# Delta-rule attention and MLP: Gram blocks written in the transpose's order, K loaded 32 wide, group 1 solved in 32 steps

## The chip, the cores and the metric

One core of a Trainium2 chip runs the whole program. The metric is the time of one execution in device microseconds; lower is better. Three runs of the kernel before took 690.51, 685.59 and 689.33 us (median 689.33). A fourth execution was profiled and took 684.56 us, of which 682.8 lie between its first and its last instruction.

## The reference, cut to what matters

```python
def _attn_ref(q, k, v, beta):                    # each (4, 8, 768, 48), beta (4, 8, 768)
    k_n = k / (np.linalg.norm(k, axis=-1, keepdims=True) + 1e-06)
    for t in range(S):
        y[:, :, t] = np.einsum('bhd,bhde->bhe', q[:, :, t], state)
        v_old = np.einsum('bhde,bhd->bhe', state, kt)
        state = state + bt[:, :, :, None] * np.einsum('bhd,bhe->bhde', kt, vt - v_old)

def _moe_ref(x, w_in, w_out):                    # x (3072, 384), w_in (384, 2048)
    h = x @ w_in
    sp = np.where(h > 20.0, h, np.log1p(np.exp(np.minimum(h, 20.0))))
    g = h * np.tanh(sp)
    return g @ w_out
```

The attention's output, with heads and width put side by side, is the `x` of the MLP.

## The kernel before

**Attention in chunks.** The 768 steps are cut into 12 chunks of 64, and two chunks make a group (g = 0 to 5). The 32 pairs of batch and head lie as two halves of 16. Within a chunk the recurrence is a triangular system. For each group the function `early(g)` builds it: TensorE multiplies K by itself (the Gram blocks, tile `pg`, L1752), VectorE masks the result out of PSUM into a tile `d` (L1755), four pieces a group, and ScalarE copies the other half of each piece to `at` (L1757). One VectorE transpose turns `d` into `gt` (L1763), so that each pair's block lies on a partition of its own. From the diagonal come the norms of K: `ss` on VectorE, then Ln and Exp on ScalarE (L1773, L1774), then a reciprocal and the factors `nb`, for which the transposed `betaT` is needed. Then the system is solved in place, on VectorE: a product `pr` (L1806) and a sum into `gt` (L1808) for each step, each of a few dozen to 256 elements a partition, each waiting for the one before.

**Two ways of solving.** `TN["fg"]` is the number of groups that are solved in two blocks of 16 steps (`split` in the code), before 2: groups 0 and 1. Their solve has 28 instructions. The blocks are then put together by TensorE in `merge(n)`, one for each chunk: matmuls `ma` (L1860, 64 a chunk), a ScalarE copy `ym` (L1862), matmuls `mb` (L1871, 64 a chunk), a VectorE sum into `tt` (L1874) and a transpose `tn` (L1876). Each of the two matmul blocks of a chunk comes in two halves by row, so that the order names `ma2`, `ma3` and `mb2`, `mb3` for the chunks of group 1. The split solve ends in the transposes `tu` (L1816) and `tt` (L1818). Groups 2 to 5 are solved in one block of 32 with 60 instructions and no merge; they end in `d<-gt` (L1825) and `tn<-gt` (L1829), and GpSimd copies the result to its place in `tt` (`place`, L1841).

**What uses it.** Per chunk n, TensorE then runs `ta` (with the solved block), `tb` (with `tn`), `gq`, `pz`, and `py` with `ps`, the output and the carried state (all L1936). `py2_0` is the first output block of chunk 2. The outputs are transposed and evicted to `x` (L2061 to L2065).

**The MLP.** An `h` tile is 18 matmuls (L2089) into one of two PSUM buffers, then a chain that alternates between ScalarE and VectorE: exp (L2103), min and add (L2104), square, ln and exp (L2105 to L2107), `e<-e,h` on VectorE (L2108, which frees the `h` buffer), a cast to `g` (L2109) and a remainder on VectorE (L2110). The second product adds up in `acc` (L2126, 12 matmuls for each `g`). The weights come as float64, read as pairs of int32, and are converted to high and low parts in the first 150 us by all engines (`convert`, L1665 to L1697).

**Loads.** K of a chunk comes in eight DMAs (`load_src`), for each half two 32 wide and two 16 wide (the width of 48 in two parts). The 16 columns beside a 16-wide part are cleared by `memset` (L1710) ahead of the load, on VectorE for chunks 0 and 1 and on GpSimd for the others.

**What sets the order.** All engines run in the order in which the program is written (`manual_schedule`). That order comes from the table `TT`, which gives each step of each piece of work (such as `early1`, `merge2`, `g1.0.0`) a position. Where several are named, as in `acc(g2.1.0)`, it is the MLP's token block, half and step.

Of the kernel before, what the change touches and what calls it, by code (L numbers as in the profile page):

```python
# [28 lines left out]
def bcast_in(ap, n):  # L29
# [21 lines left out]
    'scale_v(0,1)': [27],
    'cv1': [35, 68, 70, 104, 119, 98, 131, 144, 145],
    'warm8.0': [36],
    'loado1': [43],
    'loadq': [47],
    'scale_v(0,0)': [48],
    'warm11.5': [49],
    'loadi2': [50],
    'loadk2': [51],
    'loado0': [52],  # L60
    'merge0': [62, 71, 99, 101],
    'loado2': [63],
    'loado5': [64],
    'loado3': [65],
    'loadi4': [66],
    'loadx': [67],
    'turn_q(0,0,(0,))': [72],
    'cv2': [73, 110, 111, 112, 165, 156, 177, 194, 178],
    'turn_q(0,1,(1,))': [74],
# [2328 lines left out]
```

## Time and profile before

| what | value |
|---|---|
| runs of the kernel | 690.51, 685.59, 689.33 us, median 689.33 |
| the profiled execution | 684.56 us; its span 682.8 us, mean granted clock 0.970 |
| TensorE (PE) busy | 635.3 us, 93% of the span |
| VectorE (DVE) busy | 489.9 us, 72% |
| ScalarE (ACT) busy | 430.3 us, 63% |
| GpSimd (POOL) busy | 72.1 us, 11% |

"Busy" is the time in which at least one instruction of the engine is under way; what is left of the span is the engine's idle time. A row of the timeline begins with start and duration in us, and ends in brackets with the idle time of the engine ahead of it and the instruction that ended that time; "issue" there means that nothing in the profile explains the wait. The granted clock is the share of full speed that TensorE was given in a stretch. An average over the span hides stages: VectorE is busy for 72% over all, but for 95% from 140 to 160 us.

### The profile page before, as it was taken

To read this page: it belongs to the slowest core of one execution; us is meant where nothing else is said; L and a number is where in the kernel's file an instruction comes from. 1 tells how busy PE (TensorE), PEld (TensorE's weight loads), DVE (VectorE), ACT (ScalarE), POOL (GpSimd) and SP (SyncE) were. 2 spreads that over 40 slices of the span, in tenths; PEclk is the share of its full clock that TensorE was granted. 3 is DMA by queue.
4 is the path that set the end of the run, shared out by engine and by line. 5 is a ranking of instruction groups with operands and counts; after the bars stand their busy time and mean duration, and the time that the engine had idled before them with its cause. 6 is when DMAs were issued, how large, how long until landed. Compare 5 with 4: busy or idle time off the path is not lost.

```text
span 682.8 us, 23514 instructions
## 1 busy us (share of the span) xinstructions
PE 635.3 (93%) x10203; PEld 577.8 (85%) x10203; DVE 489.9 (72%) x1042; ACT 430.3 (63%) x802; POOL 72.1 (11%) x119
## 2 busy tenths in 40 slices
...
GB/s 154 164 285 216 213 1 26 1 48 49 5 48 49 64 19 45 62 22 56 36 33 53 45 35 42 48 37 26 42 42 35 22 42 48 25 20 7 1 24 23
DMA packets 161510, 37.79 MB, mean 55 GB/s; under 512 B 154720, under 2 KB 157792, under 8 KB 161408
## 3 DMA queue, kind: packets, MB, share of 16 engines
...
q10 hardware_dynamic: 6464, 0.69, 0.8%
...
## 4 chain that ended last, share of the span: by engine, by line
PE 43%; DVE 35%; ACT 8%; issue 6%; DMA 4%; SPq 4%; ACTq 0%; DVEq 0%
PE h L2089 15%; PE acc L2126 15%; DVE gt L1808 5%; DVE pr L1806 5%; DVE e L2108 4%; DVE g L2110 3%; SPq L1621 3%; DVE xx L1987 3%; PE gq L1936 3%; DVE xx L1923 2%; DMA kt<-in_k_dram 2%; DVE gt L1763 2%; DVE e L2104 2%; DMA xx<-in_q_dram 2%; PE pg L1752 2%
## 5 line engine op out<-in xcount | busy, mean ns | idle before, releaser
L2089 PE MATMUL h<-x,wi 128*128 128x256 f32 x1728 | 232.1, 289 | 17.3 <-DVE e L2108 5.4
L2089 PEld LDWEIGHTS h<-x,wi 128*128 128x128 f32 x1728 | 218.9, 192 | 25.2 <-DVE e L2108 6.7
L2126 PE MATMUL acc<-wo,g 128*128 128x384 f32 x1152 | 225.5, 344 | 4.4 <-DVE g L2110 2.2
L2126 PEld LDWEIGHTS acc<-wo,g 128*128 128x128 f32 x1152 | 199.8, 190 | 10.8 <-DVE g L2110 6.1
L2108 DVE SCALAR_TENSOR_TENSOR e<-e,h 128x512 f32<-128x512 f32 x96 | 65.7, 684 | 76.8 <-ACT e L2107 75.3
L2105 ACT ACTIVATE e<-e 128x512 f32<-128x512 f32 x96 | 60.6, 631 | 54.1 <-DVE e L2104 53.3
L2109 ACT CAST g<-e 128x512 fp32r<-128x512 f32 x96 | 59.3, 618 | 48.5 <-DVE e L2108 47.0
L2110 DVE TENSOR_TENSOR g<-e,g 128x512 fp32r<-128x512 f32 x96 | 68.4, 713 | 28.8 <-ACT g L2109 27.7
L2103 ACT ACTIVATE e<-h 128x512 f32<-128x512 f32 x96 | 57.2, 595 | 42.7 <-PE h L2089 34.2
L2107 ACT ACTIVATE e<-e 128x512 f32<-128x512 f32 x96 | 60.6, 632 | 2.7
L2106 ACT ACTIVATE e<-e 128x512 f32<-128x512 f32 x96 | 60.6, 631 | 2.5
L2104 DVE TENSOR_SCALAR e<-e 128x512 f32<-128x512 f32 x96 | 41.6, 435 | 26.2 <-ACT e L2103 25.8
L1808 DVE TENSOR_TENSOR gt<-gt,pr 128x84 f32<-128x84 f32 (+14 forms) x148 | 51.3, 346 | 3.5
L1806 DVE TENSOR_TENSOR pr<-gt 128x84 f32<-128x84 f32 (+14 forms) x148 | 49.8, 337 | 3.5
L1936 PE MATMUL gq<-xx,kt 48*64 48x112 f32 (+1 forms) x768 | 44.5, 260 | 2.2 <-DVE xx L1923 1.3
L1936 PE MATMUL py<-xx 128*64 128x48 f32 x768 | 43.5, 227 | 2.9 <-ACT xx L2009 2.9
L1936 PEld LDWEIGHTS py<-xx 128*64 128x64 f32 x768 | 39.5, 141 | 7.8 <-ACT xx L2009 3.8
L1936 PEld LDWEIGHTS gq<-xx,kt 48*64 48x64 f32 x768 | 38.3, 136 | 4.4 <-DVE xx L1923 2.2
L1987 DVE TENSOR_TENSOR xx<-gq,amask 64x256 f32<-64x256 f32 x96 | 40.2, 418 | 0.7
L1936 PE MATMUL ps<-xx 128*48 128x48 f32 x704 | 39.0, 211 | 0.4 <-DVE xx L1987 0.2
L1936 PEld LDWEIGHTS pz<-vt,tt 64*64 64x64 f32 x768 | 32.7, 135 | 5.1 <-issue 2.9
L1936 PE MATMUL pz<-vt,tt 64*64 64x48 f32 x768 | 36.6, 231 | 0.0
...
## 6 DMA issues: line engine op xcount, KB each, us to landing
...
kt<-in_k_dram SPq DMA_DIRECT2D x44, 64.0 KB, 2.5
...
```

The lines of the kernel that those rows point to most:

```text
L1806: nc.vector.tensor_tensor(out=pv, in0=nj, in1=xj, op=ALU.mult)
L1808: nc.vector.tensor_tensor(out=below, in0=below, in1=pv, op=ALU.add)
L1936: last[:] = [nc.tensor.matmul(*a, start=True, stop=True)]
L1987: nc.vector.tensor_tensor(out=x[r, p4, hh, D:D + C], in0=ps[r, :, d:], in1=bcast_mid(amask[r], 4), op=ALU.mult)
L2089: nc.tensor.matmul(h[:, f2, :], wt["i", f * P // WI * NCH + c][:, i2, f0:f0 + P], x[:, c, :], start=(i == 0), stop=(i == 3 * NCH - 1))
L2105: (0.65, lambda: nc.scalar.activation(e, e, AF.Square)),
L2106: (0.65, lambda: nc.scalar.activation(e, e, AF.Ln, bias=0.5, scale=0.5)),
L2107: (0.7, lambda: nc.scalar.activation(e, e, AF.Exp, scale=-1.0)),
L2108: (0.8, lambda: nc.vector.scalar_tensor_tensor(e, e, -1.0, h, op0=ALU.add, op1=ALU.mult)),
L2109: (0.7, lambda: nc.scalar.copy(out=gg[:, 0], in_=e)),
L2110: (0.8, lambda: eng.tensor_tensor(out=gg[:, 1], in0=e, in1=gg[:, 0], op=ALU.subtract))):
L2126: nc.tensor.matmul(acc[t], gg[:, a, f2, ts_], wt["o", f][:, i2, :], start=(f == 0 and i == 0), stop=(f == NF - 1 and i == 2))
```

## The change

1. For groups that are solved in 32 steps the masked Gram block is written to `d` in the order in which the transpose reads it, so that `gt<-d` reads contiguously; `tn` is transposed from the solved `d`, again contiguously, and no more from `gt`.
2. The 16-wide parts of K (and of Q's chunk 1) are loaded 32 wide, with the first 16 values of the row that follows in memory (`wide_rows`); nothing uses these values. Of the 24 memsets of `kt` only the last chunk's remain, and the two of `q1` go.
3. `fg` is 1: group 1 is solved in 32 steps, like groups 2 to 5. `merge2` and `merge3` are gone; group 1 gets the `d<-gt`, `tn<-d` and placing copies of the later groups, and `ta2` reads `d`.
4. The table `TT` is new throughout (1415 keys for 1425).

```diff
-    TN = dict(tl=4.0, fg=2, pl=[*range(0, 8)], po=8, pg=(), db=2, sp=21, slow=1.4, ab0=(39.5, 1.45), gqe=(2.,2.), ev=0,
+    TN = dict(tl=4.0, fg=1, pl=[*range(0, 8)], po=8, pg=(), db=2, sp=21, slow=1.4, ab0=(39.5, 1.45), gqe=(2.,2.), ev=0,
...
+    def wide_rows(src, hh):
+
+        flat = src.rearrange("hh t (b h) d -> (hh b h t d)", b=2)
+        rows = flat[32:B * H * S * D - (D - 32)].rearrange("(m d) -> m d", d=D)
+        m0 = hh * (NP * S - C)
+        return rows[m0:m0 + NP * S, 0:32].rearrange("(p t) d -> t p d", t=S)
...
+                if ch and n == NS - 1:
+                    nc.gpsimd.memset(dst[64 * (1 - hh) + 32:64 * (1 - hh) + 64, :, :, D - 32:], 0.0)
...
-                    load(dst[r0:r0 + 32, :, tb, :w], src[hh, t0:t0 + 32, :, 32 * ch:32 * ch + w])
+                    if ch and n < NS - 1:
+
+                        load(dst[r0:r0 + 32, :, tb, :], wide_rows(src, hh)[t0 + C * hh:t0 + C * hh + 32])
+                    else:
+                        load(dst[r0:r0 + 32, :, tb, :w], src[hh, t0:t0 + 32, :, 32 * ch:32 * ch + w])
...
-        for r in (slice(32, 64), slice(96, 128)):
-            (nc.vector if n < 2 else nc.gpsimd).memset(kts[n][r, :, :, D - 32:], 0.0)
...
+        dg = dt.rearrange("p a b f -> p (a b f)").rearrange("p (f a b) -> p a b f", a=2, b=NP)
...
-                    nc.vector.tensor_tensor(out=dt[:, t2, pr, :], in0=ps[:, :, 32:],
+                    to = dt[:, t2, pr, :] if split else dg[:, t2, pr, :]
+                    nc.vector.tensor_tensor(out=to, in0=ps[:, :, 32:],
...
-        nc.vector.transpose(gt, dt.rearrange("p a b f -> p f (a b)"))
+        if split:
+            nc.vector.transpose(gt, dt.rearrange("p a b f -> p f (a b)"))
+        else:
+            nc.vector.transpose(gr.rearrange("p a b -> p (a b)")[:, :32 * 32], dt.rearrange("p a b f -> p (a b f)"))
...
-            nc.vector.transpose(tn.rearrange("p a b j -> p j (a b)"), gt.rearrange("p i j -> p j i"))
+            nc.vector.transpose(tn.rearrange("p a b j -> p (a b j)"), dt.rearrange("p a b i -> p (a b i)"))
...
-    put(f"early{1}", early(1), *TN['e1'], *spread(us(1 + TN['s1'][0]), us(1 + TN['s1'][1]), 28), us(1 + TN['f1']), need=("K2",))
-    put(f"merge{2}", merge(2), *(us(1 + t) for t in TN['m2']), need=(f"T{(2) // 2}",))
-    put(f"merge{3}", merge(3), *(us(1 + t) for t in TN['m3']), need=(f"T{(3) // 2}",))
+    put(f"early{1}", early(1), *TN['e1'], *spread(us(1 + TN['s1'][0]), us(1 + TN['s1'][1]) + 10, 60), *(us(1 + TN['s1'][1]) + 11 + i for i in range(4)), need=("K2",))
...
-    'loada': [5],
+    'loada': [53],
```

What the new table does is seen in the order of the engines. First ScalarE, from its first instruction that is no load on: before, one load of its function table stands ahead of the copies to `at` and of Ln and Exp (L1773, L1774), and the copy of `betaT` behind them.

```order
L2200 ACT_TABLE_LOAD
L1757 COPY at_151<-pg_1_185 128x256
L1757 COPY at_151<-pg_0_152 128x256
L1757 COPY at_219<-pg_0_220 128x256
L1757 COPY at_219<-pg_1_261 128x256
L1773 ACTIVATE y_320<-ss_318 128x32
L1774 ACTIVATE y_320<-y_320 128x32
L2191 COPY betaT<-beta 128x192
```

The same place in the changed kernel, where Ln and Exp are L1779 and L1780.

```order
L1760 ACT_TABLE_LOAD
L1760 COPY at_154<-pg_0_155 128x256
L1760 COPY at_154<-pg_1_188 128x256
L1760 COPY at_228<-pg_0_229 128x256
L2197 COPY betaT<-beta 128x192
L1760 COPY at_228<-pg_1_264 128x256
L1779 ACT_TABLE_LOAD
L1779 ACTIVATE y_326<-ss_324 128x32
L1780 ACT_TABLE_LOAD
L1780 ACTIVATE y_326<-y_326 128x32
```

The step that asks for the joint table (`loada`) now comes later than these instructions, so three loads stand here instead of one, two of them between the last copy and Exp; a fourth, the joint table, follows further on (L2206). The second place is VectorE at the end of group 1's solve. Before, the 28 instructions end in L1808, and then:

```order
L1810 TENSOR_TENSOR gt_1954<-gt_1954,bp_2022 128x2x16x16
L1816 STREAM_TRANSPOSE tu_2286<-gt_1954 128x16x32
L1818 STREAM_TRANSPOSE tt_102<-gt_1954 128x32x32
L2104 TENSOR_SCALAR e_1_2260<-e_1_2260 128x512
L1721 STREAM_TRANSPOSE kt_1263<-kt_1263 128x1024
L2108 SCALAR_TENSOR_TENSOR e_1_2260<-e_1_2260,h_1_2241 128x512
L1874 TENSOR_TENSOR tt_102<-tt_102,mb_0_2397 128x8x16
L2104 TENSOR_SCALAR e_2_2310<-e_2_2310 128x512
L1874 TENSOR_TENSOR tt_102<-tt_102,mb_1_2435 128x8x16
```

In the changed kernel 60 instructions end in L1814, and then:

```order
L1816 TENSOR_TENSOR gt_1991<-gt_1991,bp_2047 128x1024
L1831 STREAM_TRANSPOSE d_1515<-gt_1991 128x32x32
L2116 TENSOR_TENSOR g_0_2180<-e_0_2179,g_0_2180 128x512
L1835 STREAM_TRANSPOSE tn_2301<-d_1515 128x1024
L2110 TENSOR_SCALAR e_1_2334<-e_1_2334 128x512
L1722 STREAM_TRANSPOSE kt_1234<-kt_1234 128x1024
L2110 TENSOR_SCALAR e_2_2266<-e_2_2266 128x512
L2114 SCALAR_TENSOR_TENSOR e_1_2334<-e_1_2334,h_1_2315 128x512
L2116 TENSOR_TENSOR g_1_2335<-e_1_2334,g_1_2335 128x512
```

The sums of the merges are gone from between the MLP's instructions, one `g` (L2116, the remainder that the second product reads) stands between the last two transposes, and the two transposes feed `ta2` and `tb2` directly.

## Rows read from the trace of the kernel before

**Rows 1.** The page, part 1: busy time of each engine, share, instructions.
```profile
PE 635.3 (93%) x10203; PEld 577.8 (85%) x10203; DVE 489.9 (72%) x1042; ACT 430.3 (63%) x802; POOL 72.1 (11%) x119
```
**Rows 2.** Windows: stretch, length, busy PE, PEld, DVE, ACT, POOL, clock, DMA, GB/s.
```profile
140.00:160.00 20.00, 14.94 (x207) 13.72 (x208) 19.08 (x50) 8.95 (x16) 0.00 (x0) 0.91 0.36 61
160.00:180.00 20.00, 18.35 (x660) 17.36 (x663) 11.02 (x19) 11.74 (x24) 4.40 (x7) 0.92 0.05 7
```
**Rows 3.** Timeline of VectorE: group 1's solve from its transpose to its end.
```profile
128.92 2.05 DVE L1763 STREAM_TRANSPOSE gt<-d 128x1024 f32<-128x1024 f32 x1
...
156.61 0.69 DVE L1810 TENSOR_TENSOR gt<-gt,bp 128x512 f32<-128x512 f32 x1
157.34 1.06 DVE L1816 STREAM_TRANSPOSE tu<-gt 128x512 f32<-128x512 f32 x1
158.30 1.90 DVE L1818 STREAM_TRANSPOSE tt<-gt 128x1024 f32<-128x1024 f32 x1
```
**Rows 4.** Timeline of TensorE from group 1's merges to the first output block.
```profile
158.54 1.27 PE L1860 MATMUL ma<-tu,d 16*32 16x16 f32 x128 [2.53 <-DVE tu L1816]
159.75 3.91 PE L2126 MATMUL acc<-wo,g 128*128 128x384 f32 x12
...
167.69 1.20 PE L1936 MATMUL ta<-tt,at 32*32 32x32 f32 x64
168.81 2.38 PE L2126 MATMUL acc<-wo,g 128*128 128x384 f32 x12
...
175.04 0.24 PE L1871 MATMUL mb<-tt,ym 32*32 32x16 f32 x5 [1.65 <-issue]
175.21 2.40 PE L2089 MATMUL h<-x,wi 128*128 128x256 f32 x18
...
186.33 0.42 PE L1871 MATMUL mb<-tt,ym 32*32 32x16 f32 x26 [1.49 <-issue]
186.68 0.32 PE L1936 MATMUL py<-xx 128*64 128x48 f32 x4
```
**Rows 5.** Windows of tile ma (PE, PEld, ACT), then of mb (PE, PEld, DVE).
```profile
155.00:190.00 35.00, 2.79 (x256) 2.55 (x256) 0.98 (x4) 0.91 0.13 21
...
155.00:190.00 35.00, 3.12 (x256) 2.66 (x256) 1.15 (x4) 0.91 0.13 21
```
**Rows 6.** Windows of tile pr, the solve's instructions: group 1, then group 2.
```profile
138.00:157.00 19.00, 7.34 (x28) 0.91 0.31 57
190.00:258.00 68.00, 20.18 (x60) 1.00 0.30 47
```
**Rows 7.** Groups by form on VectorE (busy us, mean ns); one timeline row, group 2.
```profile
L1721 DVE STREAM_TRANSPOSE kt<-kt 128x1024 f32<-128x1024 f32 x12 | 14.9, 1240 | 3.0 <-DMA kt<-in_k_dram 2.9
L1829 DVE STREAM_TRANSPOSE tn<-gt 128x1024 f32<-128x1024 f32 x4 | 8.9, 2221 | 0.6 <-PE ta L1936 0.6
...
193.11 1.22 DVE L1790 TENSOR_TENSOR gt<-gt,nb 128x1024 f32<-128x1024 f32 x1
```
**Rows 8.** Group by form on ScalarE, and VectorE's timeline behind group 0's solve.
```profile
L2200 ACT ACT_TABLE_LOAD x1 | 1.3, 1283 | 7.1 <-DMA kt<-in_k_dram 7.1
...
33.20 0.71 DVE L1923 STREAM_TRANSPOSE xx<-xx 64x512 f32<-64x512 f32 x1
```
**Rows 9.** Timeline of TensorE: group 0's mb, ta0, tb0 and the first output.
```profile
41.00 1.30 PE L1871 MATMUL mb<-tt,ym 32*32 32x16 f32 x82 [1.81 <-issue]
...
45.27 0.69 PE L1936 MATMUL ta<-tt,at 32*32 32x32 f32 x18 [1.10 <-issue]
...
51.80 1.20 PE L1936 MATMUL tb<-at,tn 32*32 32x32 f32 x64
...
58.66 0.32 PE L1936 MATMUL py<-xx 128*64 128x48 f32 x2 [0.57 <-ACT xx L2009]
```
**Rows 10.** Waits of TensorE from 187 us on: total us, times, longest.
```profile
PE h L2089 <- DVE e L2108: 4.6, 6, 1.9
PE acc L2126 <- DVE g L2110: 2.2, 4, 0.7
```

More of the change, by code (lines that the diff above doesn't have):

```diff
@@ L51 @@
[L51 to L69, printed above, removed]
@@ new lines @@
+    'early0.1>1': [10],
+    'early0.2>1': [11],
+    'loado2': [12],
+    'loadi1': [15],
+    'loads': [17],
+    'early0.4>1': [18],
+    'turn_beta()': [19],
+    'early0.5>1': [20],
+    'warm8.0': [22],
+    'warm11.5': [24],
+    'loado1': [25],
+    'loadq': [26],
+    'scale_v(0,0)': [27],
+    'cv0': [50, 28, 62, 81, 84, 108, 112, 129, 128],
+    'scale_v(0,1)': [30],
+    'cv1': [31, 52, 61, 92, 106, 85, 130, 139, 140],
+    'loadi2': [34],
+    'loadk2': [37],
+    'cv4': [38, 57, 156, 158, 219, 227, 230, 231, 192],
@@ new lines @@
+    'loada': [53],
+    'turn_q(0,1,(0,))': [54],
+    'turn_q(0,0,(1,))': [55],
+    'loado3': [59],
+    'turn_q(0,0,(0,))': [60],
+    'loado5': [63],
+    'loadi4': [64],
+    'loadx': [65],
+    'loado6': [76],
+    'loado0': [77],
+    'loadi3': [78],
+    'warm30.6': [79],
+    'warm29.5': [80],
+    'merge0': [82, 83, 99, 100],
+    'loado4': [86],
+    'loadi5': [87],
+    'loadp': [88],
+    'gq00': [89],
+    'cv5': [90, 144, 194, 195, 196, 211, 215, 223, 216],
+    'turn_q(0,1,(1,))': [91],
@@ new lines @@
+    'g1.0.6': [456],
+    'g1.0.7.0>1': [457],
+    'ats_y[1,1].0>1': [459],
+    'scale_v(2,0)': [461],
+    'g1.0.6.0>1': [465],
+    'scale_v(2,1)': [466],
+    'g1.0.6.0>2': [467],
+    'g2.0.5': [478],
+    'turn(1,)': [479],
+    'g1.0.6.0>3': [480],
+    'g1.0.6.0>4': [481],
+    'g1.0.6.0>5': [482],
+    'turn(1,).0>3': [483],
+    'ats_gq[2,0]': [484],
+    'turn(1,).0>1': [490],
+    'g1.0.6.0>6': [492],
+    'g1.0.6.0>7': [496],
+    'turn(1,).0>4': [499],
+    'turn(1,).0>2': [510],
@@ new lines @@
+    'g1.0.7.0>2': [518],
+    'g1.0.6.0>8': [524],
+    'g1.1.0': [525],
+    'turn_q(2,1)': [529],
+    'prep(3,)': [530],
+    'g2.0.6': [538],
+    'g1.1.0.0>1': [539],
+    'g1.0.7.0>3': [540],
+    'g1.0.7.0>4': [541],
+    'g1.0.7.0>5': [542],
+    'g1.0.7.0>6': [543],
+    'g1.1.0.0>2': [553],
+    'g1.0.7.0>7': [555],
+    'g1.0.7.0>8': [562],
+    'g1.1.2': [567],
+    'ats_gq[2,0].0>1': [570],
+    'ats_gq[2,0].0>2': [576],
+    'g1.1.0.0>3': [578],
+    'g1.1.0.0>4': [579],
+    'g1.1.0.0>5': [580],
@@ new lines @@
+    'g1.1.0.0>6': [583],
+    'g1.1.0.0>7': [588],
+    'g1.1.0.0>8': [589],
+    'g1.1.2.0>1': [590],
+    'g2.0.7': [592],
+    'g1.1.1': [593],
+    'g2.0.7.0>1': [594],
+    'g2.0.7.0>2': [595],
+    'g2.1.0': [596],
+    'g1.1.1.0>1': [597],
+    'g1.1.1.0>2': [598],
+    'g1.1.1.0>3': [600],
+    'g1.1.1.0>4': [601],
+    'ats_a[2]': [602],
+    'g1.1.1.0>5': [603],
+    'g1.1.2.0>2': [604],
+    'g1.1.2.0>3': [605],
+    'g1.1.1.0>6': [606],
+    'g1.1.1.0>7': [607],
+    'ats_a[2].0>1': [608],
@@ new lines @@
+    'g1.1.1.0>8': [609],
+    'g1.1.2.0>4': [610],
+    'g1.1.3': [611],
+    'g1.1.2.0>5': [612],
+    'g1.1.2.0>6': [613],
+    'g2.1.1': [614],
+    'g1.1.3.0>1': [615],
+    'g1.1.2.0>7': [618],
+    'g1.1.2.0>8': [619],
+    'g1.1.3.0>2': [620],
+    'ats_b[2]': [621],
+    'g1.1.3.0>3': [623],
+    'g1.1.3.0>4': [624],
+    'g1.1.4': [625],
+    'ats_b[2].0>1': [626],
+    'scale_v(3,1)': [629],
+    'g1.1.3.0>5': [630],
+    'g1.1.3.0>6': [631],
+    'g1.1.3.0>7': [632],
+    'g1.1.4.0>1': [633],
@@ new lines @@
+    'g1.1.5.0>8': [702],
+    'g1.1.6.0>5': [703],
+    'g1.1.7': [704],
+    'ats_y[2,1].0>1': [706],
+    'g1.1.6.0>6': [708],
+    'turn(2,)': [709],
+    'g1.1.6.0>7': [710],
+    'ats_b[3]': [714],
+    'g1.1.7.0>1': [715],
+    'turn(2,).0>1': [716],
+    'turn(2,).0>3': [719],
+    'g1.1.6.0>8': [720],
+    'turn(2,).0>4': [722],
+    'turn(2,).0>2': [724],
+    'g1.1.7.0>2': [725],
+    'g1.1.7.0>3': [727],
+    'g1.1.7.0>4': [728],
+    'turn_q(3,1)': [730],
+    'prep(4,)': [731],
+    'ats_b[3].0>1': [732],
@@ new lines @@
+    'g2.1.7.0>1': [765],
+    'g1.2.0.0>6': [766],
+    'ats_y[3,0]': [767],
+    'g1.2.1.0>2': [769],
+    'g1.2.0.0>7': [770],
+    'g2.1.7.0>2': [773],
+    'g1.2.0.0>8': [774],
+    'g1.2.3': [776],
+    'g1.2.1.0>3': [778],
+    'g1.2.1.0>4': [779],
+    'g1.2.1.0>5': [782],
+    'scale_v(4,0)': [783],
+    'g2.2.0': [784],
+    'ats_y[3,0].0>1': [785],
+    'g1.2.1.0>6': [789],
+    'g1.2.1.0>7': [790],
+    'g1.2.3.0>1': [791],
+    'g1.2.1.0>8': [795],
+    'g1.2.3.0>2': [797],
+    'early3.3>1': [801],
@@ new lines @@
+    'g1.2.2': [804],
+    'g1.2.3.0>3': [805],
+    'g1.2.3.0>4': [809],
+    'g1.2.3.0>5': [810],
+    'g2.2.1': [811],
+    'g1.2.2.0>1': [812],
+    'g1.2.3.0>6': [813],
+    'g1.2.2.0>2': [814],
+    'g1.2.3.0>7': [815],
+    'turn_q(4,0)': [816],
+    'early3.2>1': [817],
+    'g1.2.2.0>3': [818],
+    'g1.2.2.0>4': [819],
+    'g1.2.3.0>8': [820],
+    'g1.2.4': [821],
+    'g1.2.2.0>5': [822],
+    'ats_z[3,1]+s_gq[4,0]': [824],
+    'ats_z[3,1]+s_gq[4,0].0>2': [825],
+    'g1.2.2.0>6': [826],
@@ new lines @@
+    'g2.2.3': [851],
+    'g1.2.5.0>3': [853],
+    'g1.2.4.0>7': [854],
+    'g1.2.5.0>4': [856],
+    'g1.2.5.0>5': [857],
+    'ats_a[4].0>1': [858],
+    'turn(3,)': [859],
+    'turn(3,).0>3': [860],
+    'g1.2.4.0>8': [862],
+    'g1.2.6': [864],
+    'turn(3,).0>1': [866],
+    'g1.2.5.0>6': [867],
+    'g1.2.6.0>1': [869],
+    'g2.2.4': [870],
+    'turn(3,).0>4': [871],
+    'turn(3,).0>2': [872],
+    'g1.2.5.0>7': [873],
+    'scale_v(4,1)': [874],
+    'g1.2.6.0>2': [878],
+    'g1.2.5.0>8': [880],
@@ new lines @@
+    'g1.2.7.0>3': [924],
+    'g1.3.0.0>6': [925],
+    'g1.2.7.0>4': [926],
+    'g1.2.7.0>5': [927],
+    'g1.2.7.0>6': [932],
+    'g1.2.7.0>7': [933],
+    'g1.2.7.0>8': [937],
+    'ats_y[4,0]': [938],
+    'scale_v(5,1)': [939],
+    'ats_y[4,0].0>1': [940],
+    'g1.3.1': [941],
+    'g1.3.0.0>7': [942],
+    'g1.3.1.0>1': [943],
+    'g1.3.0.0>8': [945],
+    'g1.3.1.0>2': [946],
+    'g2.2.7': [950],
+    'g2.2.7.0>1': [951],
+    'g1.3.1.0>3': [953],
+    'g1.3.1.0>4': [954],
+    'g1.3.1.0>5': [955],
@@ new lines @@
+    'g1.4.3.0>2': [1129],
+    'g1.4.3.0>3': [1130],
+    'g1.4.4': [1131],
+    'g1.4.3.0>4': [1133],
+    'g1.4.3.0>5': [1134],
+    'g2.4.2': [1136],
+    'g1.4.4.0>1': [1139],
+    'g1.4.3.0>6': [1143],
+    'g1.4.3.0>7': [1144],
+    'g1.4.4.0>2': [1147],
+    'g1.4.4.0>3': [1148],
+    'g1.4.3.0>8': [1151],
+    'g1.4.5': [1152],
+    'ats_y[5,1]': [1153],
+    'g1.4.4.0>4': [1154],
+    'g1.4.4.0>5': [1155],
+    'g1.4.5.0>1': [1157],
+    'g1.4.4.0>6': [1160],
+    'g2.4.3': [1162],
+    'g1.4.4.0>7': [1163],
@@ new lines @@
+    'g1.5.7.0>4': [1359],
+    'g1.5.7.0>5': [1361],
+    'g1.5.6.0>8': [1362],
+    'g1.6.0': [1363],
+    'g1.6.0.0>1': [1364],
+    'g2.5.6': [1365],
+    'g1.5.7.0>6': [1366],
+    'g1.6.0.0>2': [1367],
+    'ats_z[7,0]+s_gq[7,1].0>1': [1368],
+    'g1.6.0.0>3': [1369],
+    'g1.5.7.0>7': [1370],
+    'g1.6.0.0>4': [1371],
+    'g1.6.0.0>5': [1372],
+    'g1.5.7.0>8': [1373],
+    'g1.6.1': [1374],
+    'g2.5.7': [1376],
+    'g1.6.0.0>6': [1377],
+    'g1.6.0.0>7': [1378],
+    'g1.6.1.0>1': [1379],
```

1178 lines of the change are left out of this document (1151 added, 27 removed), and 1372 rows, old and new, of the table TT.

## The prediction

> **What bounds the kernel now.** I read the page first: TensorE (PE) is busy for 93% of the span, VectorE (DVE) for 72% [rows 1]. On that alone one would say that only TensorE's work counts. Then I read the windows of 20 us: from 140 to 160 us VectorE is busy for 19.08 of 20 us and TensorE for 14.94, and in the next 20 us it is the other way round, 11.02 and 18.35 [rows 2]. So the stretch in which the change puts the longer solve has VectorE as its limit until 160 us, and slack on VectorE behind it. The timeline shows what ends there: group 1 is transposed at 128.92 us, and its solve ends with `tt` at 158.30 + 1.90 = 160.20 us [rows 3]. That is 31.3 us, in which VectorE also serves the MLP and converts weights. TensorE waits 2.53 us for `tu`, then runs the merges among MLP work, `ta2` at 167.69 and the first output block of chunk 2, `py2_0`, at 186.68 us, with idle times of 1.65 and 1.49 us ahead of two of the merges' blocks, for which the trace names no instruction [rows 4]. From there the two kernels have the same work on TensorE. I therefore ask when `py2_0` starts in the changed kernel, and what is different behind it.
>
> **What goes.** Group 1's merges hold TensorE for 2.79 + 3.12 = 5.91 us [rows 5], and the three idle times beside them add 2.53 + 1.65 + 1.49 = 5.67 us [rows 4]. At most 11.6 us of TensorE can come free. The memsets of `kt` lie on GpSimd, which is 11% busy [rows 1], or ahead of the first K; I give them nothing, since the work of TensorE behind them starts with K's landing and not with them. If a later K load had waited for GpSimd's memset, there would be a wait of `pg` for it; none of the large waits is one [rows 10], so the bound is about zero on both sides. The 16-wide loads become 32 wide, with as many packets; I give that nothing, for DMA is 36% busy or less at the loads of chunk 3 and later [rows 2].
>
> **What group 1's solve costs.** Its own instructions took 7.34 us in 28 steps; group 2's 60 took 20.18 us [rows 6]: +12.84. The two products with a factor for each row or column are twice as large, 1.22 for 0.69 us each [rows 3, 7]: +1.06. `d<-gt` takes the place of `tu` and `tt`: a transpose with one strided side takes 2.05 us [rows 3], against 1.06 + 1.90: -0.91. The transpose into `gt` now reads contiguously: the one contiguous transpose of this size takes 1.24 us [rows 7], so -0.81. Together 31.3 + 12.84 + 1.06 - 0.91 - 0.81 = 43.5 us from `gt` to `d`, as VectorE is full and other work stands between the steps as before (the order has about as much of it). If VectorE's idle time of that stretch, some 5% [rows 2], is used up, it is 42; so 42 to 43.5, and I take 43.5, since the steps alternate with chains that ScalarE must feed.
>
> **From there to py2_0.** On VectorE a remainder `g` stands right behind `d` (as VectorE's order shows), 0.7 us for its 512 elements as for L1810 [rows 3]; the second product `acc` that waits for it stands ahead of `ta2` on TensorE. That `acc` takes 2.38 us, or 3.91 where TensorE had idled just before it: the same 12 matmuls [rows 4]. In the changed kernel TensorE has little to do for about 20 us ahead of it, since its `h` and `acc` blocks wait for instructions of VectorE that stand between the steps; so 3.9. `ta2` starts at 43.5 + 0.7 + 3.9 = 48.1 us behind `gt`, where it started at 167.69 - 128.92 = 38.8. From `ta2` to `py2_0` it took 186.68 - 167.69 = 19.0 us. Of that go the idle 1.65 + 1.49 and the merge blocks that lie there, 0.7 + 0.8 + 0.9 (a half of `ma` is 0.7 us at 2.79 / 4, a half of `mb` 0.8 at 3.12 / 4, the last a little more), and one `h` block more stands there, 2.40 us [rows 4, 5]: 15.9 us. So `py2_0` comes 64.0 us behind `gt`, where it came 57.8: **+6.2 us**. If all runs at full clock and VectorE's idle time is used, it is +3; if two blocks more run at the slow rate and their `e` chains are late by as much, +9.
>
> **What comes earlier.** Ahead of `gt` two things pull in opposite ways. The order of ScalarE shows two loads of its function table between the last copy and Exp, one of them ahead of Ln, where it may lie beside VectorE's transpose. A load took 1.283 us [rows 8]. One load is on the chain for certain, so +1.3 to +2.6; I take 2.1, since the copy of `betaT` has moved ahead of them too. Into group 0's solve VectorE now takes three transposes of `xx`, 0.71 us each [rows 8], and five conversions of 0.3 to 0.4 us, where it had one: +3.6. Against that, `tb0` stood 51.80 - 45.96 = 5.8 us behind the end of `ta0`, with eight warm-up matmuls and four of a conversion between them [rows 9]. In the new order only two of the latter are left there, and the warm-ups stand behind `tb0`: -3.6. The `gq` blocks no longer wait for those transposes, which have run by then: -2.0. Together +0.1, so that the first output block stays at about 58.7 us [rows 9]; bounds -3 (the unexplained idle times of 1.81 and 1.10 us go too [rows 9]) and +3 (both loads on the chain and half of these shifts lost). Then half of a merge of chunk 1 stands behind the first `h`, not ahead of it, 0.7 us by [rows 5], and between the first `e` of the MLP and `gt` of group 1 VectorE's order holds 47.1 us of work by the mean of each form, for 49.5. So `gt` starts 3.0 us earlier, and `py2_0` is late by 6.2 - 3.0 = **+3.2 us**.
>
> The Trainium skill ("ScalarE: Activation LUTs", section "What ACT_TABLE_LOAD costs") gives about 1283 ns for the load, as the trace, and a drain of about as long again with it, 2.66 us for a switch. No drain can be seen in this trace, which has one load at the start. By the Trainium skill the sum would be higher by about 2.8 us for two such loads on the chain, an estimate from that section.
>
> **What comes back behind py2_0.** In groups 2 to 5 the transpose into `gt` gives 0.81 us each, `tn` 2.22 - 1.24 = 0.98 [rows 3, 7]: 1.8 us of VectorE a group, 7.2 in all. The masked evictions, four a group, now write with a stride. The trace has no such instruction. Below, it costs nothing, as the trace has no reason for a loss in a two-input operation; above, what a stride costs a transpose, 0.81 us per 1024 elements, so 0.2 for 256 and 0.8 a group. I take half. Then 5.6 us of VectorE are saved, off the path except where TensorE waits for VectorE: the two largest waits of that stretch are 4.6 and 2.2 us [rows 10]. I give the change **-2.5 us** there, with bounds 0 and -5. The work that hides the rest is TensorE's MLP, which is full.
>
> The Trainium skill ("SBUF — State Buffer", section "Specifications (TRN2)") has lines of 16 bytes, with a penalty for each step to a new line. By that section's rule the evictions, which step 128 bytes, would pay the upper bound, and the first part of the change would only move the price of `gt` from the transpose to the evictions. The sum would then be +1 us higher. The strided transposes agree with the rule: 2.05 for 1.24 us.
>
> **The sum.** +3.2 - 2.5 = +0.7 us. The profiled execution took 684.56 us, so 685.3 for one like it. The three runs have a median of 689.33, and the mean of all four is 687.5; the sum on that is 688.2. I predict **688 us**, about the same. About 1% (6.9 us) is what a measurement of this kernel can tell from no change.
>
> **Rivals.** (A) *The merges come out whole.* If the longer solve hides in VectorE's slack, the 11.6 us of TensorE go: 687.5 - 11.6 = 676. For it: VectorE is idle for 9 of 20 us right behind the solve [rows 2], and the early bound of -3. Against: the slack lies behind the solve, and `ta2` stands behind it. A middle form, with half of them, gives 681. (B) *The solve is the new bound and the clock falls with it* (the other side). VectorE's extra 12.2 us up to `d` lie ahead of `ta2`; TensorE waits, and the `h` and `acc` blocks behind the wait run at the slow rate, 1.5 us more each [rows 4]. With +9 there, no gain ahead and none behind: 687.5 + 9 = 696.5. It decides from `py2_0` at 193.6 us on, if nothing comes back later. For it: 19.08 of 20 us [rows 2]. Against: only three blocks stand there. (C) *The parts ahead of `gt` go wrong*: table loads, full solve, late K, +3 each side of nothing: 691 to 692, no verdict. That the change doesn't do what it says is excluded by the order of the instructions.
>
> **Chances.** Forecast with (C), 682.4 to 696.2 us: 0.52. (A), below: 0.31. (B), above: 0.17. The range goes from 676 to 698, from all of (A) to a little above (B); the likeliest case by itself has 683 to 694.
>
> **What would show it.** Right: no `ma2`, `mb2`; 60 steps in about 20 us; `gt` of group 1 near 126 us, `d` 42 to 44 us behind it, `ta2` near 174 and `py2_0` near 190; Ln about 2 us later behind `ss`, with loads of 1.28 us; `gt` and `tn` transposes at 1.24 us. Wrong: `py2_0` ahead of 184 (A) or behind 193 (B); evictions at more than 0.6 us; idle time of TensorE behind `py2_0` that differs by more than 5 us.

## The result, and the profile after

The changed kernel takes 682.04 us (median of 10 runs, 677.92 to 685.82), the kernel before 688.68 us on the same chip (10 runs, 685.59 to 690.51). The ratio is **0.9894, with an interval of 0.9865 to 0.9923**: faster by 1.1%, where "about the same" was forecast at 688 us. The profiled execution took 679.45 us, 5.1 us less than that of before.

The page of the changed kernel, part 1, beside [rows 1]:

```profile
PE 625.0 (92%) x9687; PEld 575.4 (85%) x9691; DVE 486.6 (72%) x1064; ACT 433.6 (64%) x801; POOL 62.8 (9%) x100
```

TensorE has 516 matmuls and 10 us of busy time less, VectorE 3 us less. The windows that answer [rows 2]:

```profile
140.00:160.00 20.00, 11.16 (x55) 10.52 (x56) 19.18 (x50) 5.83 (x10) 0.00 (x0) 0.79 0.03 5
160.00:180.00 20.00, 15.21 (x234) 13.73 (x236) 15.55 (x30) 9.69 (x17) 6.59 (x9) 0.87 0.26 47
```

VectorE is as full as before until 160 us and for longer behind it (15.55 us for 11.02), and TensorE stands still for almost 9 of the 20 us, where it stood for 5. So this stretch got worse. VectorE's timeline, for [rows 3]:

```profile
126.19 1.24 DVE L1769 STREAM_TRANSPOSE gt<-d 128x1024 f32<-128x1024 f32 x1
...
167.13 2.02 DVE L1831 STREAM_TRANSPOSE d<-gt 128x1024 f32<-128x1024 f32 x1
...
169.57 1.22 DVE L1835 STREAM_TRANSPOSE tn<-d 128x1024 f32<-128x1024 f32 x1
```

Group 1 starts 2.7 us earlier, and 43.0 us lie from `gt` to the end of `d`. TensorE's timeline, for [rows 4]:

```profile
165.31 3.91 PE L2095 MATMUL h<-x,wi 128*128 128x256 f32 x18 [3.63 <-DVE e L2114]
169.05 0.51 PE L2132 MATMUL acc<-wo,g 128*128 128x384 f32 x2
169.72 2.02 PE L2132 MATMUL acc<-wo,g 128*128 128x384 f32 x10 [0.15 <-DVE g L2116]
171.67 1.20 PE L1942 MATMUL ta<-d,at 32*32 32x32 f32 x64
173.87 2.40 PE L2095 MATMUL h<-x,wi 128*128 128x256 f32 x18 [1.00 <-DVE e L2114]
...
185.71 2.26 PE L1754 MATMUL pg<-kt 48*32 48x64 f32 x64 [1.82 <-issue]
...
192.81 0.32 PE L1942 MATMUL py<-xx 128*64 128x48 f32 x4
```

`py2_0` starts at 192.8 us, 6.1 us later than before. The span ends 5.1 us earlier. So between these two executions the changed kernel loses 6 us up to this block and gains 11 behind it; how much of the 6 is chance is seen below. The granted clock around the block, from two windows of 5 us (the number ahead of the DMA share):

```profile
185.00:190.00 5.00, 4.29 (x116) 4.15 (x118) 2.65 (x6) 2.07 (x5) 0.00 (x0) 0.58 0.01 3
190.00:195.00 5.00, 5.00 (x173) 4.58 (x171) 2.88 (x6) 2.15 (x5) 0.00 (x0) 0.74 0.01 3
```

TensorE ran for some of this time at the lower of its two levels, 1.2 GHz, after the idle time of 1.82 us; the kernel before has 0.72 and 0.94 in the same two windows. Behind 193 us its waits are smaller than [rows 10]:

```profile
PE h L2095 <- DVE e L2114: 2.1, 3, 0.9
PE h L2095 <- DVE x L2071: 1.4, 2, 1.3
PE acc L2132 <- DVE g L2116: 1.3, 3, 0.5
```

The rest of the document asks where those 11 us come from. One table serves for this. From each trace I take the first matmul of `py2_0`, that of `py6_0` (the first output block of chunk 6) and the end of TensorE's work. "Order" says whose table of positions holds behind `py2_0`.

| kernel | order behind | parts | py2_0 at | py2_0 to py6_0 | py6_0 to end | ratio to before |
|---|---|---|---|---|---|---|
| before | old | none | 186.7 | 193.4 | 298.3 | 1 |
| changed | new | all | 192.8 | 185.2 | 295.3 | 0.9894 |
| b_edits12 | old | 1, 2 | 191.8 | 192.8 | 296.3 | 1.0002 |
| b_fg1 | old | 1, 2, 3 | 199.0 | 191.7 | 297.3 | 1.0125 |
| a_fg2 | new | 1, 2 | 196.8 | 186.8 | 295.8 | 0.9929 |
| a_table | new | all | 192.9 | 185.2 | 298.0 | 0.9901 |
| h_oldfront | new | 1, 2 | 189.9 | 184.5 | 298.0 | 0.9831 |
| h_newfront | old | all | 193.5 | 192.2 | 297.0 | 1.0005 |
| a_oldwrite | new | 2, 3 | 192.7 | 185.9 | 296.3 | 0.9910 |
| a_memset | new | 1, 3 | 190.8 | 185.2 | 297.6 | 0.9900 |
| h_mid | new to py6_0 | 1, 2 | 191.7 | 187.9 | 298.1 | 0.9897 |
| b_accswap | old, 12 blocks moved | 1, 2 | 193.6 | 195.9 | 299.6 | 1.0125 |
| h_three | new | 1, 2 | 185.8 | 187.7 | 297.5 | 0.9818 |
| b_rear | new | none | 191.8 | 187.3 | 296.8 | 0.9852 |

The ratios are of 6 to 12 runs of each changed kernel; the three columns of times are of one execution each. A run more than 1.5% above the fastest of its kernel counts as slow and is left out of the ratio; for b_rear these are 7 of 12 runs, the traced one among them, and with all 12 its ratio (of the means) is 0.990.

The start of the program scatters. b_edits12, h_oldfront, h_mid and b_accswap have the same instructions in the same order up to `py2_0`, and reach it between 189.9 and 193.6 us; the kernel before and b_rear share theirs as well, and reach it at 186.7 and 191.8. So the trace of the kernel before is the earliest of six with the old front, whose mean is 190.9 us. The five executions with the changed kernel's order up to there (changed, a_table, a_oldwrite, a_memset, h_newfront) have a mean of 192.5. The loss ahead of `py2_0` is thus nearer to 2 us than to 6. What scatters lies ahead of `gt` of group 1 (128.9 to 134.4 us in the old front); from there to `py2_0` the old front takes 57.4 to 59.8 us and the changed one 64.1 to 66.6. The stretch from `py2_0` to `py6_0` repeats itself far better. Its windows, in the kernel before, b_edits12 and the changed kernel:

```profile
186.68:380.08 193.40, 182.27 (x3024) 170.61 (x3019) 171.27 (x382) 122.34 (x228) 25.59 (x39) 0.99 0.27 43
191.85:384.67 192.82, 182.06 (x3025) 171.15 (x3020) 168.20 (x383) 122.32 (x228) 20.17 (x29) 0.99 0.28 47
192.81:377.99 185.18, 177.49 (x3025) 169.15 (x3019) 163.60 (x378) 123.37 (x231) 20.01 (x28) 1.00 0.29 49
```

With the same matmuls, TensorE stands still for 11.1, 10.8 and 7.7 us there, so less than half of the 8 us is idle time. The rest is a shorter busy time. The granted clock of 0.99 accounts for up to 2 us of that, by an estimate from these rows; what makes the remainder isn't shown.

### The profile page after: what moved, and what is told of

Read it like the earlier page. It is cut to its first block, busy times and chain, and to the rows that moved or that the text cites. A ratio compares the mean times of both kernels' runs of the same rounds, so it can differ in the third digit from the quotient of the medians.

```text
span 677.7 us, 22475 instructions
## 1 busy us (share of the span) xinstructions
PE 625.0 (92%) x9687; PEld 575.4 (85%) x9691; DVE 486.6 (72%) x1064; ACT 433.6 (64%) x801; POOL 62.8 (9%) x100
## 3 DMA queue, kind: packets, MB, share of 16 engines
q8 instruction: 76, 1.25, 0.8%
## 4 chain that ended last, share of the span: by engine, by line
PE 58%; DVE 26%; issue 5%; SPq 4%; DMA 4%; ACT 3%; DVEq 0%; ACTq 0%
PE h L2095 22%; PE acc L2132 20%; SPq L1611 4%; DVE pr L1812 4%; DVE gt L1814 4%; PE gq L1942 3%; PE py L1942 3%; DVE e L2114 2%; DVE xx L1993 2%; DVE g L2116 2%; DMA kt<-in_k_dram 2%; DMA xx<-in_q_dram 2%; PE pg L1754 1%; PE pz L1942 1%; PE ps L1942 1%
## 5 line engine op out<-in xcount | busy, mean ns | idle before, releaser
L2132 PE MATMUL acc<-wo,g 128*128 128x384 f32 x1152 | 222.4, 342 | 7.4 <-DVE g L2116 6.6
L2116 DVE TENSOR_TENSOR g<-e,g 128x512 fp32r<-128x512 f32 x96 | 67.4, 703 | 30.6 <-ACT g L2115 29.8
L2110 DVE TENSOR_SCALAR e<-e 128x512 f32<-128x512 f32 x96 | 43.0, 448 | 32.6 <-ACT e L2109 32.1
L1812 DVE TENSOR_TENSOR pr<-gt 128x58 f32<-128x58 f32 (+9 forms) x164 | 56.4, 344 | 4.1
L1814 DVE TENSOR_TENSOR gt<-gt,pr 128x58 f32<-128x58 f32 (+9 forms) x164 | 54.1, 330 | 3.3
L1942 PE MATMUL py<-xx 128*64 128x48 f32 x768 | 42.1, 224 | 1.9 <-ACT xx L2015 1.8
L1929 DVE STREAM_TRANSPOSE xx<-xx 64x512 f32<-64x512 f32 x44 | 31.1, 706 | 10.1 <-DMA xx<-in_q_dram 8.2
L1918 POOL TENSOR_TENSOR vt<-vt,ne 128x384 f32<-128x384 f32 x24 | 22.6, 951 | 161.0 <-DMA vt<-in_v_dram 98.9
```

The source lines that it names most:

```text
L1812: nc.vector.tensor_tensor(out=pv, in0=nj, in1=xj, op=ALU.mult)
L1814: nc.vector.tensor_tensor(out=below, in0=below, in1=pv, op=ALU.add)
L1942: last[:] = [nc.tensor.matmul(*a, start=True, stop=True)]
L2116: (0.8, lambda: eng.tensor_tensor(out=gg[:, 1], in0=e, in1=gg[:, 0], op=ALU.subtract))):
L2132: nc.tensor.matmul(acc[t], gg[:, a, f2, ts_], wt["o", f][:, i2, :], start=(f == 0 and i == 0), stop=(f == NF - 1 and i == 2))
```

## The experiments

### Parts 1 and 2 alone: b_edits12

```diff
-    nc.vector.tensor_tensor(out=dt[:, t2, pr, :], in0=ps[:, :, 32:],
+    to = dt[:, t2, pr, :] if split else dg[:, t2, pr, :]
+    nc.vector.tensor_tensor(out=to, in0=ps[:, :, 32:],
...
-    (nc.vector if n < 2 else nc.gpsimd).memset(kts[n][r, :, :, D - 32:], 0.0)
```

> The kernel before with parts 1 and 2 alone (Gram blocks written in the transpose's order, K loaded 32 wide), two-block solve of group 1 and the old order kept. Theory V (VectorE's relief of about 1 us a group, 0.77 from each gt transpose and 0.98 from each tn less 4 x 0.19 for the evictions, ends waits of TensorE behind py2_0): 4 us or more below the kernel before, 682 to 685, with TensorE's idle time behind 190 us smaller by 3 us or more. Theory O (what came back behind py2_0 comes from the new written order): within 2 us of the kernel before, 686.5 to 690, idle time behind 190 us as before.

Measured: 686.72 us, ratio 1.0002 (0.9967 to 1.0037). Theory O holds in the time. In the trace there is a little of theory V: 489.1 us from `py2_0` to the end for 491.7, 2.6 us less and near the 2.5 us that the prediction gave to VectorE's relief (b_fg1 and h_newfront, with the same parts and order there, have 489.0 and 489.3); in the time it doesn't show. TensorE's waits behind 193 us, of b_edits12:

```profile
PE h L2105 <- DVE e L2124: 3.6, 7, 1.3
PE acc L2142 <- DVE g L2126: 1.9, 3, 0.7
PE gq L1952 <- DVE x L2081: 1.4, 1, 1.4
```

They are nearly those of before: 3.6 and 1.9 us where [rows 10] have 4.6 and 2.2.

### Group 1 in 32 steps in the old order: b_fg1

```diff
-    TN = dict(tl=4.0, fg=2, ...
+    TN = dict(tl=4.0, fg=1, ...
...
-    'early1': [133, 289, 342, 351, 359, 387, 453, 466, 478, 481, 483, 486, ...
+    'early1': [133, 289, 342, 351, 359, 387, 453, 466, 478.0, 479.373, 480.746, 481.746, ...
```

> The same, and group 1 solved in 32 steps: the old order with its 28 solve positions stretched over the same places to 60, merges of group 1 gone. Theory S (the longer solve delays ta2 by more than the merges give back): 3 to 6 us above the run with parts 1 and 2 alone, py2_0 at 190 to 194 us. Theory G (the merges' 11.6 us of TensorE come out in the end): 4 to 10 us below it, py2_0 at 180 to 186 us.

Measured: 695.97 us, ratio 1.0125 (1.0084 to 1.0165), 9 us above b_edits12; `py2_0` at 199.0 us. Theory S holds in its sign, but the price is larger than its 3 to 6 us, and `py2_0` is later than its 190 to 194. TensorE's timeline of b_fg1 shows where:

```profile
163.23 3.92 PE L2105 MATMUL h<-x,wi 128*128 128x256 f32 x18 [4.50 <-DVE e L2124]
...
178.14 4.21 PE L2105 MATMUL h<-x,wi 128*128 128x256 f32 x18 [8.88 <-DVE e L2124]
182.28 1.92 PE L1952 MATMUL ta<-d,at 32*32 32x32 f32 x64
```

Two `h` tiles wait 13.4 us for an `e` that VectorE reaches late, since solve steps stand ahead of it, and then run at the slow rate (3.92 and 4.21 us for 2.40). This is rival (B) of the prediction, in the order before. The places of the 60 steps are mine, stretched over the old ones, so the price is that of an order not made for them.

### Two blocks in the new order: a_fg2

```diff
-    TN = dict(tl=4.0, fg=1, ...
+    TN = dict(tl=4.0, fg=2, ...
...
+    'merge2': [588, 589, 595, 598],
+    'merge2.0>1': [590],
+    'merge2.1>1': [592],
...
+    'merge3': [603.5, 622, 622.5, 645],
```

> The changed kernel with group 1 solved in two blocks again: the new order, with 28 of its 60 solve positions and the merges put between its blocks as the old order had them. Theory S: py2_0 back at about 186 to 188 us and the time 3 to 6 us below the changed kernel, 676 to 679. Theory G: the merges cost again what they cost before, 4 to 10 us above the changed kernel, 686 to 692.

Measured: 681.79 us, ratio 0.9929 (0.9893 to 0.9965). Neither theory holds as it was put. The solve has 32 instructions less, and `py2_0` doesn't come earlier, but at 196.8 us; still the kernel is faster than before by 0.7%: from `py2_0` to `py6_0` it takes 186.8 us, as kernels in the new order do. Against the changed kernel's 0.9894 the intervals overlap: part 3 is worth nothing that could be measured in the new order, where in the old it costs 1.25%. Here too the places, those of the merges, are mine, so what part 3 is worth in an order made for it isn't shown.

### The function table at the front: a_table

```diff
-    'loada': [53],
+    'loada': [6.5],
```

> The changed kernel with the joint function table of ScalarE asked for at the front again, so that one load stands ahead of the first copy and none between the copies, Ln and Exp. If the two loads on the chain ahead of group 0's solve cost what the trace shows (2 x 1.28 us) and that start is on the path: 2.5 us below the changed kernel, 679.5, with ta0 and py0 earlier by 2.6 to 3 us. If what follows hides them (waits for weights between 90 and 145 us): no difference, 681 to 683. The Trainium skill (ScalarE: Activation LUTs, section What ACT_TABLE_LOAD costs) has a drain with each load; by it the chain would be shorter by some 5 us, an estimate from that section.

ScalarE's timeline of the changed kernel shows what there is to take away:

```profile
17.05 0.38 ACT L1760 COPY at<-pg 128x256 f32<-128x256 f32 x1
17.44 1.28 ACT L1779 ACT_TABLE_LOAD   x1
18.74 0.23 ACT L1779 ACTIVATE y<-ss 128x32 f32<-128x32 f32 x1
18.98 1.28 ACT L1780 ACT_TABLE_LOAD   x1
20.28 0.23 ACT L1780 ACTIVATE y<-y 128x32 f32<-128x32 f32 x1
```

and that of a_table:

```profile
16.86 0.38 ACT L1760 COPY at<-pg 128x256 f32<-128x256 f32 x1
17.98 0.23 ACT L1779 ACTIVATE y<-ss 128x32 f32<-128x32 f32 x1 [0.73 <-DVE ss L1777]
18.24 0.23 ACT L1780 ACTIVATE y<-y 128x32 f32<-128x32 f32 x1
```

Exp starts 2.0 us earlier. Measured: 680.25 us, ratio 0.9901 (0.9864 to 0.9939), as the changed kernel. What follows hides it: the merge of group 0 starts 0.4 us earlier (37.01 for 37.43 us), and `py0` isn't earlier at all (64.1 for 62.9 us). The loads take 1.28 us each, and Ln starts 0.02 us behind one; a drain as in the Trainium skill ("ScalarE: Activation LUTs", section "What ACT_TABLE_LOAD costs") isn't seen here.

### Old front, new rear, and the reverse: h_oldfront, h_newfront

Both number the whole table anew. In h_oldfront all steps up to `ats_y[2,0]` keep the old order, and those behind it come in the new one; three lines of 1400:

```diff
 'ats_y[2,0]': [633],
-'g2.2.0': [762],
+'g2.2.0': [765],
-'g2.2.2': [812],
+'g2.2.2': [819],
```

> Parts 1 and 2 with the two-block solve of group 1 in the old order up to py2_0 (the step ats_y[2,0]), and the new order behind it. Theory O2 (the new order gains only behind py2_0, 6 to 9 us, and loses ahead of it): py2_0 at 187 to 192 us as in the run with parts 1 and 2 alone, then 485 to 487 us to the end, 676 to 680 in all, ratio to the kernel before 0.985 to 0.990. Theory B (the new order gains only as one whole, since its rear is fitted to its front): 484 us are not reached behind py2_0, 684 or more, ratio 0.995 to 1.005.

> The changed kernel with its order up to py2_0 and the old order behind it. Theory O2: py2_0 at 192 to 193 us as in the changed kernel, then 489 us or so as in the run with parts 1 and 2 alone; 3 to 4 us above the kernel before, ratio 1.003 to 1.008. Theory F (it is the work ahead of py2_0, the missing merges, that gives the gain later): the time of the changed kernel, ratio 0.987 to 0.992.

Measured: h_oldfront 676.63 us, ratio **0.9831 (0.9787 to 0.9875)**; h_newfront 687.87 us, 1.0005 (0.9974 to 1.0036). Theory O2 holds in its sign on both sides, with ratios a little below its ranges. The new order behind `py2_0` gives 1.7% behind the old front (b_edits12 has 1.0002) and 1.1% behind the changed kernel's (0.9894 for 1.0005); that front, with the merges gone, gives nothing. Waits of h_oldfront behind 190 us:

```profile
PE h L2105 <- DVE e L2124: 2.2, 3, 1.0
PE gq L1952 <- DVE xx L1939: 2.0, 2, 1.8
```

No wait of `acc` is left among the large ones.

### Without part 1, without part 2: a_oldwrite, a_memset

```diff
-                    to = dt[:, t2, pr, :] if split else dg[:, t2, pr, :]
-                    nc.vector.tensor_tensor(out=to, in0=ps[:, :, 32:],
+                    nc.vector.tensor_tensor(out=dt[:, t2, pr, :], in0=ps[:, :, 32:],
```

> The changed kernel without part 1: masked Gram blocks written contiguously, gt and tn transposed with a stride. VectorE gets 1.0 us a group back on it, 5 us in five groups (the evictions 0.18 us each shorter, gt 0.77 and tn 0.98 longer). If VectorE's relief is what TensorE waits for behind py2_0: 3 to 5 us above the changed kernel, ratio to the kernel before 0.994 to 0.997. If the order's slack hides it: within 2 us of the changed kernel, 0.988 to 0.992.

```diff
+        for r in (slice(32, 64), slice(96, 128)):
+            (nc.vector if n < 2 else nc.gpsimd).memset(kts[n][r, :, :, D - 32:], 0.0)
```

> The changed kernel without part 2: K loaded 16 wide beside cleared corners, memsets back on VectorE for chunks 0 and 1 and on GpSimd for the others. If the memsets cost nothing and the additional bytes neither: within 2 us of the changed kernel, ratio to the kernel before 0.987 to 0.992. If the additional 1.4 MB hold up the start, where DMA is 90% busy: py0 earlier by 1.5 us or more than in the changed kernel, and 1 to 3 us below it. If GpSimd's memsets hold up later loads: 2 us or more above it.

Measured: 681.05 us, ratio 0.9910 (0.9876 to 0.9943), and 680.44 us, 0.9900 (0.9866 to 0.9934). Both are as fast as the changed kernel. The groups by form of the changed kernel say what part 1 does on VectorE:

```profile
L1758 DVE TENSOR_TENSOR d<-pg,lmask 128x256 f32<-128x256 f32 x24 | 13.9, 577 | 11.4 <-PE pg L1754 11.3
...
L1769 DVE STREAM_TRANSPOSE gt<-d 128x1024 f32<-128x1024 f32 x5 | 6.2, 1243 | 0.1
L1835 DVE STREAM_TRANSPOSE tn<-d 128x1024 f32<-128x1024 f32 x5 | 6.2, 1237 | 0.1
```

and those of a_oldwrite:

```profile
L1764 DVE STREAM_TRANSPOSE gt<-d 128x1024 f32<-128x1024 f32 x6 | 12.0, 2008 | 0.2
L1830 DVE STREAM_TRANSPOSE tn<-gt 128x1024 f32<-128x1024 f32 x5 | 11.2, 2233 | 0.1
L1756 DVE TENSOR_TENSOR d<-pg,lmask 128x256 f32<-128x256 f32 x24 | 9.9, 412 | 9.3 <-PE pg L1753 9.3
```

The transposes are 0.77 and 1.00 us shorter, but all evictions together take 4.0 us more. What `gt` saves (12.0 less 6.2 and the 1.9 of group 0, 3.9 us) the evictions pay back; only `tn` is a gain, 5 us in all.

### The new order in one stretch: h_mid

As h_oldfront, but the old order again behind `ats_y[6,0]`.

> Parts 1 and 2, two-block solve, the old order up to py2_0, the new order from there to the output blocks of chunk 6 (ats_y[6,0]), and the old order again behind. Traces so far: between py3_0 and py6_0 the new order needs 149 us for the same work that takes 155 us in the old; behind py6_0 they differ by 2 us or less. Theory M (the gain lies in that stretch): 7 to 9 us below the kernel before, ratio 0.986 to 0.991, py6_0 earlier than in the old order by 6 to 8 us counted from py2_0. Theory E (it is spread to the end): ratio 0.991 to 0.996.

Measured: 679.46 us, ratio 0.9897 (0.9858 to 0.9936). From `py2_0` to `py6_0` it takes 187.9 us, where the kernels in the old order take 191.7 to 193.4; behind it the times lie between 295.3 and 298.3 us in either order (b_accswap aside). Theory M holds in the time, with 4.9 us from `py2_0` to `py6_0` (against b_edits12) where it had 6 to 8: in the stretch in which groups 3 to 5 are built beside the MLP lies a gain of 1%. The 0.7% by which h_oldfront is ahead of it is within the two intervals.

### Only TensorE's blocks moved: b_accswap

```diff
-    'g2.2.0': [762],
+    'g2.2.0': [775],
```

Twelve blocks of the second product, such as `g2.2.0`, come behind the next block of TensorE.

The reason for it is a place like this one in the kernel before:

```profile
226.77 0.62 PE L2126 MATMUL acc<-wo,g 128*128 128x384 f32 x2 [0.60 <-ACT g L2109]
228.06 2.03 PE L2126 MATMUL acc<-wo,g 128*128 128x384 f32 x10 [0.67 <-DVE g L2110]
```

The block waits for the first half of `g`, runs two matmuls and waits again. In the changed kernel its blocks run in one piece there:

```profile
226.30 2.27 PE L2132 MATMUL acc<-wo,g 128*128 128x384 f32 x12
```

> Parts 1 and 2, two-block solve and the old order, but twelve blocks of the second product behind py2_0, those that in the old order start before or within 0.3 us of the end of the remainder g that they read, each moved behind the next block of TensorE. Theory A (TensorE waits because these blocks stand too early in the order): idle time ahead of acc behind 193 us falls from 3.2 us to under 1, 3 to 6 us below the run with parts 1 and 2 alone, ratio to the kernel before 0.991 to 0.996. Theory N (a block put later only moves the wait to the next h or to VectorE): ratio 0.997 to 1.003.

Measured: 695.40 us, ratio 1.0125 (1.0076 to 1.0173), the slowest with b_fg1. Theory A falls, and N with it, since it is worse than no difference. TensorE's waits behind 193 us, of b_accswap:

```profile
PE pg L1764 <- DVE kt L1732: 4.1, 2, 2.9
PE gq L1952 <- DVE x L2081: 4.0, 1, 4.0
PE h L2105 <- DVE e L2124: 3.0, 5, 1.3
PE py L1952 <- ACT xx L2025: 2.2, 4, 1.4
PE xt L2077 <- ACT yy L2054: 1.9, 1, 1.9
```

The waits of `acc` are gone, as theory A said. In their place stand waits of 4.1 and 4.0 us, of `pg` and `gq`, for blocks whose inputs VectorE and ScalarE still make in the old order.

### New, old, new: h_three

The new order also up to `ats_y[1,0]`, the old from there to `ats_y[2,0]`, then the new.

> As the run with the old order up to py2_0 and the new behind it, but with the new order up to py1_0 (ats_y[1,0]) too: new, old, new. The new order took 36 to 38 us from py0 to py1, the old 40 to 45; the old took 85 from py1 to py2, the new 92 to 94. If the stretches add up: 3 to 6 us below the run with the old front, 671 to 674 by the kernel before at 687.7, ratio 0.974 to 0.979. If the start of chunk 1 in the new order is bought with work put off into the next stretch: the same as that run or slower, ratio 0.982 to 0.990.

Measured: 674.71 us, ratio **0.9818 (0.9766 to 0.9871)**. It has the lowest median, but against h_oldfront the difference is within the intervals, and neither case of the expectation is decided: what the new order gives up to `py1_0` (38.4 us from `py0` to `py1`, for 44.3 in h_oldfront) isn't clear of noise in the time.

### The order alone: b_rear

The kernel before, with nothing changed but the order behind `ats_y[2,0]`.

> The kernel before with nothing but the new order behind py2_0 (ats_y[2,0]): no part 1, no part 2, two-block solve. The run with parts 1 and 2 beside this order had a ratio of 0.983 and took 482 us from py2_0 to the end. If the order alone does it: ratio 0.979 to 0.988, 482 to 485 us behind py2_0 (up to 2.6 us more without VectorE's relief), and py2_0 at 187 to 190 us. If the new order needs the shorter transposes to be worth it: 487 us or more behind py2_0, ratio 0.990 or above.

Measured: ratio 0.9852 (0.9809 to 0.9895), or 0.990 with all of its 12 runs. It has the same table of positions as h_oldfront, and only parts 1 and 2 are missing. From `py2_0` to the end it takes 484.2 us, within the 482 to 485 expected of the order alone, for 482.5 in h_oldfront and 491.7 in the kernel before. So the order gives 1.0 to 1.5% by itself: parts 1 and 2 aren't needed for the gain. Whether they add to it (0.983 in h_oldfront) isn't clear of noise.

## Why the prediction was right and where it was wrong

The time lies in the range of 676 to 698 us, but not in the way that the sum had it: +0.7 us by the sum, -5.1 in the profiled execution, -6.6 in the medians. With 682.04 us it is just below the likeliest case (682.4 to 696.2) and so in the band of rival (A), whose mechanism didn't happen. The range was kept by luck in part: a gain that the sum didn't have was large enough to change the verdict, but not to leave the range.

- **From gt to d:** 43.5 us by the sum, 43.0 measured (42.9 to 43.7 in the other traces with the new order there). The step that costed the solve by [rows 6] held to half a microsecond.
- **Start of gt:** 3.0 us earlier by the sum, 2.7 measured, but by chance in part: over the executions named below the table the means are 132.5 us in the old front and 126.7 in the new, 5.8 earlier. `py0` was to stay at 58.7 us and came at 62.9, with an idle time of 4.18 us within `ta0` that has no named cause (the kernel before had 1.10 there [rows 9]). The next stretch, from `py0` to `py1`, took 36.2 us for 42.6 and gave it back. The two table loads were both on the chain, 2.6 us where 2.1 were taken, and a_table shows that this is hidden in any case.
- **From d to py2_0:** `ta2` came 45.5 us behind `gt`, not 48.1: the `acc` ahead of it had begun at 169.05, before the end of `d` at 169.15, and was not at the slow rate. From `ta2` on it took 21.1 us for 15.9. The term was too low by 5 us, since it took these blocks without new waits and at full clock: an `h` waited 1.00 us more, a `pg` 1.82, and the blocks after that ran at 0.58 and 0.74 of full clock. From `gt` to `py2_0` the change costs 8.9 us between the two profiled executions (66.6 for 57.8) and 7.4 between the means of the executions named, for the +6.2 of the sum and within its +3 to +9. `py2_0` itself is 6.1 us late between the two and 1.6 between the means, for the +3.2 of the sum: up to here the sum is as good as the scatter lets one see.
- **Behind py2_0:** this step failed. The prediction wrote "From there the two kernels have the same work on TensorE" and gave -2.5 us for VectorE's relief. The work is the same, and b_edits12 has the -2.6 us in its trace. But the changed kernel gains 11.2 us there, and 6 to 9 of them (489.1 us of b_edits12 less 482.5 of h_oldfront; 489.3 of h_newfront less 480.4) come from the written order, which had no term in the sum. It was treated as a carrier of the other parts. h_oldfront and b_rear show that it is the gain, and h_newfront that without it nothing is left. One of the prediction's own signs of being wrong pointed here: TensorE's idle time behind `py2_0` is 10.4 us for 15.5, where 5 us of difference was the limit.
- **Evictions:** half of the upper bound was taken, 0.1 us each; they take 0.602 us in the median for 0.417, which is the whole bound (0.19), and with 0.602 us just over the 0.6 that the prediction had as a sign of being wrong. The rule of the Trainium skill on 16-byte lines ("SBUF — State Buffer", section "Specifications (TRN2)"), by which part 1 would only move the price of `gt`, is what the trace shows.
- **Rivals:** (A), the merges' 11.6 us, didn't happen: part 3 costs 1.25% in the old order and gives nothing clear of noise in the new, with places of mine in both. (B) is what part 3 does with an order that isn't made for it.

What stays open: which engine's order gives the gain between `py2_0` and `py6_0`. VectorE is busy there for 171.3 us before, 168.2 in b_edits12 and 163.6 in the changed kernel, which is 87 to 89% of the stretch each time. b_accswap shows only that moving twelve blocks of TensorE doesn't do it; TensorE's whole new order with the old one on the other engines wasn't tried, nor VectorE's and ScalarE's alone. Open too is what ends the idle times that the trace calls "issue", 4.18 us in the largest case.
